# Hidden layer on mirrored token pairs: the first product by 64-row tiles, ReLU as two maxima on VectorE

## The chip, the cores and the metric

One core of one Trainium2 chip. The kernel before took 452.25 us (median of two runs, 452.08 to 452.43).

Engines are called as the profile calls them: PE is TensorE, PEld its weight loads, DVE is VectorE, ACT is ScalarE, POOL is GpSimd, SP is SyncE.

## The reference

```python
x = inputs['x']                                # (8, 3136, 256) float32
X = np.fft.fft(np.fft.fft(x, axis=1), axis=2).real   # real part of a 2-D transform
h = X.transpose(0, 2, 1) @ U @ V               # rank 32, along the sequence
u = X + h.transpose(0, 2, 1)
out = u + np.maximum(u @ w_ch1, 0.0) @ w_ch2   # 256 -> 1024 -> 256
```

Batches are taken in four pairs. The transform is done by matmuls in two stages (the *first transform* over one factor of the sequence, the *lines* over the other), then comes the hidden layer. Two facts carry the change. Token k and its mirror, token -k modulo 3136, have transforms that agree in the even part over the 256 features and differ in the sign of the odd part. And relu(A+B) = max(A, -B) + B, relu(A-B) = max(A, B) - B.

## The kernel before

A chunk is 512 tokens. It is taken through the first product (W1), a ReLU that ScalarE writes straight into the operand of the second product, the second product (W2) with the residual added in the same accumulator, and a drain, which takes the sum out of PSUM (the memory that matmuls accumulate in). A step of the next pair's first transform is also shown.

```python
def mlp1(ch, jp):                                   # a quarter of a chunk's first product
    ...
    ps = psh.tile([P, 2, 512], FP32, tag="h", name="hps")
    for i in range(2):
        j = ...
        for blk in range(2):                        # 128 rows each: the whole array
            nc.tensor.matmul(ps[:, i, 0:n], (W1p if ch.sg > 0 else W1m)[jp // 2][:, blk, j],
                             q[:, blk, c0:c0 + n], start=(blk == 0), stop=(blk == 1))
    nc.scalar.activation(ch.h[:, 2 * jp:2 * jp + 2, 0:n], ps[:, :, 0:n], AF.Relu)

def mlp2(ch, t, last=False):                        # second product of 128 tokens
    ...
    for j in range(JT):                             # JT = 8 blocks of 128 hidden units
        nc.tensor.matmul(ps, ch.h[:, j, t * P:(t + 1) * P], W2[:, j, :], ...)
        if j < 2:                                   # residual
            nc.tensor.matmul(ps[:, j], q[:, j, tk], (Bp if ch.sg > 0 else Bm)[:, j], ...)
    ...
    def drain():
        nc.scalar.copy(om[:, 0:n], ch.po[:, 0:n, 1])
        nc.vector.tensor_tensor(ob[:, 0:n, 0:P], ch.po[:, 0:n, 0], om[:, 0:n], op=AL.add)
        nc.vector.tensor_tensor(ob[:, 0:n, P:D], ch.po[:, 0:n, 0], om[:, 0:n], op=AL.subtract)
        ...                                         # stores

def step(g):                                        # first transform of the next pair, 16 steps
    ps = psd.tile([P, 2, D], FP32, tag="ps", name="ps")    # one PSUM tile a step
    ...                                             # matmuls into ps
    evac(z[...], ps[:])                             # always ScalarE
```

## Time and profile before

| | before |
|---|---|
| time, us | 452.25 |
| PE, DVE, ACT busy, share of the span | 95%, 50%, 65% |
| granted PE clock | 1.00 throughout |
| start to first hidden product, us | 28.0 |
| pairs one, two, three, us | 114.0, 102.0, 102.3 |
| last pair and tail, us | 103.3 |

The groups of the page that the change replaces (columns: line, engine, operation, output and inputs, shapes, count, then busy us and mean ns of one, then the engine's idle time before them and what ended most of it):

```profile
L385 ACT ACTIVATE hT<-hps 128x1024 bf16<-128x1024 f32 (+1 forms) x208 | 202.6, 976 | 109.6 <-PE hps L383 100.9
L394 PE MATMUL ops<-W,hT 128*128 128x256 bf16 x1568 | 224.7, 273 | 1.2 <-DVE ob L408 1.0
```

ScalarE waits for TensorE before its ReLUs (100.9 us in all), while TensorE waits 1.2 us in the whole run before second products. Everything queues behind TensorE, so that is the engine that one wants to relieve.

### The profile page before, as it was taken

The page shows a single profiled execution, that of the slowest core. Times are in us where ns is not written, and L with a number is a line of the kernel's source. Part 1 is how long each engine was busy: PE and PEld are TensorE (multiplying, and loading weights), DVE is VectorE, ACT ScalarE, POOL GpSimd, SP SyncE. Part 2 cuts the span into 40 slices and gives each one's busy share as a digit, 9 for nine tenths or more (in the row PEclk, how much of TensorE's full clock was granted, in tenths as well). Part 3 has the DMA queues.
Part 4 walks back from the last instruction along what each step waited for, and adds up shares of the span by engine and source line. Part 5 has one row for each costly group of instructions (what it writes and reads, how often), then busy time and mean ns, then how long its engine had stood idle before and what let it go on. Part 6 is the DMA issues. An engine that isn't in the chain of part 4 may idle for free.

```text
span 449.6 us, 10536 instructions
## 1 busy us (share of the span) xinstructions
PE 426.6 (95%) x4158; PEld 308.7 (69%) x4221; DVE 224.6 (50%) x541; ACT 290.3 (65%) x402; POOL 142.6 (32%) x180
## 2 busy tenths in 40 slices
PE   3889997999999999999999999999999999999995
PEld 1756665776777777767867777777867777667764
DVE  7873686874344466373354467363354344222222
ACT  5886754676565567777465667777466655666662
POOL 7465455851330545550510545360500000000000
PEclk9999999999999999999999999999999999999999
DMA  8749753875592657863772647773662222222323
GB/s 149 159 138 168 211 162 109 254 181 176 162 231 66 171 137 214 235 207 96 171 195 62 171 113 238 223 200 101 165 141 66 71 65 66 72 72 74 85 54 93
DMA packets 59761, 64.34 MB, mean 143 GB/s; under 512 B 12950, under 2 KB 52672, under 8 KB 59552
## 3 DMA queue, kind: packets, MB, share of 16 engines
q1 hardware_dynamic: 50000, 42.68, 36.8%
q0 software_dynamic: 7232, 14.30, 13.5%
q10 hardware_dynamic: 2480, 6.69, 4.0%
q8 instruction: 33, 0.54, 0.5%
q14 instruction: 16, 0.13, 0.1%
HBM read 34.62 MB, written 32.19 MB: 149 GB/s over the span
## 4 chain that ended last, share of the span: by engine, by line
PE 84%; DVE 5%; DMA 3%; issue 3%; POOL 2%; ACT 1%; SPq 1%; DVEq 0%; ACTq 0%; POOLq 0%
PE ops L394 35%; PE hps L383 35%; PE ps L322 5%; PE ops L397 4%; PE ps L185 2%; DMA out_dram<-ob 2%; PE teps L284 1%; DMA w_f<-in_moe_w_ch_dram 1%; SPq L412 1%; DVE g L76 1%; ACT hT L385 1%; PE w1ps L679 1%; DVE q L76 0%; DVE ta L447 0%; DVE ob L407 0%
## 5 line engine op out<-in xcount | busy, mean ns | idle before, releaser
L385 ACT ACTIVATE hT<-hps 128x1024 bf16<-128x1024 f32 (+1 forms) x208 | 202.6, 976 | 109.6 <-PE hps L383 100.9
L394 PE MATMUL ops<-W,hT 128*128 128x256 bf16 x1568 | 224.7, 273 | 1.2 <-DVE ob L408 1.0
L394 PEld LDWEIGHTS <-hT 128*128 128x128 bf16 x1568 | 145.1, 98 | 35.0 <-DVE ob L408 0.8
L76 DVE CAST q<-ps 128x512 bf16<-128x512 f32 (+3 forms) x121 | 65.2, 560 | 83.8 <-PE ps L322 80.1
L383 PE MATMUL hps<-q,W1p 128*128 128x512 bf16 (+1 forms) x420 | 103.2, 355 | 2.6 <-DVE q L76 0.5
L407 DVE TENSOR_TENSOR ob<-ops,om 128x256 f32<-128x256 f32 (+1 forms) x102 | 41.8, 410 | 117.7 <-ACT om L406 116.3
L383 PE MATMUL hps<-q,W1m 128*128 128x512 bf16 x351 | 95.7, 379 | 2.1 <-ACT hT L385 0.5
L144 POOL TENSOR_TENSOR y<-xa,xb 98x510 f32<-98x510 f32 (+1 forms) x48 | 60.9, 1289 | 108.5 <-DMA xa<-in_x_dram 84.2
L383 PEld LDWEIGHTS <-W1p 128*128 128x128 bf16 x448 | 40.3, 98 | 27.3 <-issue 2.2
L383 PEld LDWEIGHTS <-W1m 128*128 128x128 bf16 x384 | 35.3, 98 | 26.5 <-issue 1.4
L397 PEld LDWEIGHTS <-q 128*128 128x128 bf16 x392 | 38.3, 98 | 21.6 <-issue 0.9
L406 ACT COPY om<-ops 128x256 f32<-128x256 f32 (+1 forms) x102 | 37.3, 366 | 14.4 <-PE ops L394 7.8
L306 POOL COPY g<-te 64x1024 int32<-64x1024 int32 (+1 forms) x23 | 24.9, 1122 | 56.3 <-DVE te L270 51.7
L408 DVE TENSOR_TENSOR ob<-ops,om 128x256 f32<-128x256 f32 (+1 forms) x102 | 41.2, 404 | 0.0
L73 ACT CAST z<-ps 128x512 bf16<-128x512 f32 x48 | 28.2, 587 | 17.2 <-PE ps L185 16.4
L397 PE MATMUL ops<-Bp,q 128*128 128x128 f16 x200 | 38.4, 219 | 0.0
L322 PE MATMUL ps<-T,g 128*128 128x128 bf16 (+3 forms) x400 | 36.9, 218 | 0.5 <-ACT q L73 0.3
L397 PE MATMUL ops<-Bm,q 128*128 128x128 f16 x192 | 36.9, 219 | 0.0
L322 PEld LDWEIGHTS <-g 128*128 128x128 bf16 (+1 forms) x400 | 29.4, 98 | 5.0 <-issue 0.6
L99 POOL DMA_INDIRECT xb<-in_x_dram,idx x24 | 25.1, 1044 | 5.4 <-issue 4.5
L134 DVE TENSOR_TENSOR yb<-y 98x508 bf16<-98x508 f32 (+1 forms) x24 | 21.1, 879 | 0.1
L76 DVE COPY g<-zt 32x400 bf16<-32x400 bf16 (+3 forms) x45 | 17.2, 383 | 6.3 <-ACT zt L73 5.7
(136 smaller groups left out, 208.1 us busy)
## 6 DMA issues: line engine op xcount, KB each, us to landing
out_dram<-ob SPq DMA_DIRECT2D x389, 64.0 KB
xa<-in_x_dram SPq DMA_DIRECT2D x24, 392.0 KB
zturn<-z ACTq DMA_DIRECT2D x9, 512.0 KB
g<-zturn SPq DMA_DIRECT2D x3, 800.0 KB
g<-zturn SPq DMA_DIRECT2D x3, 544.0 KB
X<-in_x_dram POOLq DMA_DIRECT2D x4, 384.0 KB, 7.7
X<-in_x_dram POOLq DMA_DIRECT2D x2, 744.0 KB
zturn<-z ACTq DMA_DIRECT2D x3, 448.0 KB
```

What stands on the lines that cost most here:

```text
L73: nc.scalar.copy(o, i)
L76: nc.vector.tensor_copy(o, i)
L99: nc.gpsimd.indirect_dma_start(out=ck.xb.rearrange("p l d -> p (l d)"), out_offset=None, in_=x_g, in_offset=bass.IndirectOffsetOnAxis(ap=i ...
L144: nc.gpsimd.tensor_tensor(ck.y[:, l0:l1, 1:256], ck.xa[:, l0:l1, 1:256], rb[:, l0:l1, 255:0:-1], op=AL.add)
L322: nc.tensor.matmul(o, lt, r, start=st, stop=True, skip_group_check=True)
L383: nc.tensor.matmul(ps[:, i, 0:n], (W1p if ch.sg > 0 else W1m)[jp // 2][:, blk, j], q[:, blk, c0:c0 + n], start=(blk == 0), stop=(blk == 1))
L385: nc.scalar.activation(ch.h[:, 2 * jp:2 * jp + 2, 0:n], ps[:, :, 0:n], AF.Relu)
L394: nc.tensor.matmul(ps, ch.h[:, j, t * P:(t + 1) * P], W2[:, j, :], start=(j == 0 and (t % 2 == 0 or last)), stop=(j == JT - 1), skip_group ...
L397: nc.tensor.matmul(ps[:, j], q[:, j, tk], (Bp if ch.sg > 0 else Bm)[:, j], start=False, stop=False, skip_group_check=True)
L406: nc.scalar.copy(om[:, 0:n], ch.po[:, 0:n, 1])
L407: nc.vector.tensor_tensor(ob[:, 0:n, 0:P], ch.po[:, 0:n, 0], om[:, 0:n], op=AL.add)
L408: nc.vector.tensor_tensor(ob[:, 0:n, P:D], ch.po[:, 0:n, 0], om[:, 0:n], op=AL.subtract)
```

## The change

The intent is to relieve it. A mirrored pair of tokens needs the even product A and the odd product B only once, each over its own 128 of the 256 transformed features. They run as 64-row tiles of the array, two at a time. VectorE forms the two maxima, the second written in reversed token order. The linear rest, plus or minus B times W2, joins the residual through a table W1 x W2 that is built at the start (`RR`). The low-rank term no longer goes through q but enters as its own small products (`TE`, `TK`). The second product is also cut into 64-row tiles, in two phases, so that the array stays in one tiling mode. The core of the diff:

```diff
-        for blk in range(2):
-            nc.tensor.matmul(ps[:, i, 0:n], (W1p if ch.sg > 0 else W1m)[jp // 2][:, blk, j], q[:, blk, c0:c0 + n], ...)
-    nc.scalar.activation(ch.h[:, 2 * jp:2 * jp + 2, 0:n], ps[:, :, 0:n], AF.Relu)
+        for blk in range(2):
+            for s in range(2):                      # even part on rows 0-63, odd part on rows 64-127
+                lt = W1z[64:P, ja] if s and blk == 0 else W1p[c][64 * s:64 * s + 64, blk, jc]
+                nc.tensor.matmul(o[s], lt, q[64 * s:64 * s + 64, blk, c0:c0 + w], ...)
+        for b, a, n, v in ch.parts:                 # low-rank term
+            for s in range(2):
+                nc.tensor.matmul(o[s][:, a:a + n], TE[ch.p % 2][b][64 * s:64 * s + 33, ja],
+                                 VZ[64 * s:64 * s + 33, b, v:v + n], ...)
+    ab = apool.tile([P, 3, 512], BF16, tag="ab", name="ab")      # apool: bufs=2
+    nc.scalar.copy(ab[:, 0:2], ps[:])                            # A and B
+    ts(ab[:, 2], ab[:, 1], -1.0, None)                           # -B, VectorE
+    nc.vector.tensor_tensor(h[:, 1], av[0], av[2], op=AL.max)
+    nc.vector.tensor_tensor(flip[0][:, :, ::-1], flip[1], flip[2], op=AL.max)   # mirrored
...
+    def phase(ha):                                  # second product, half the rows for each of two sides
+        ...
+        for j in range(JT):
+            for s, op, half in sides:
+                last = nc.tensor.matmul(op, ch.h[rows[half], s, j, ...], W2[rows[half], j, :], ...)
...
         def step(g):                                # first transform
-            ps = psd.tile([P, 2, D], FP32, tag="ps", name="ps")
+            if g % 2 == 0:
+                pr.s1 = bank2("s1")                 # one tile for two steps
+            ps = pr.s1[:, g % 2].rearrange("p (l d) -> p l d", l=2)
...
-            evac(z[...], ps[:])
+            evac[g % 2](z[...], ps)                 # ScalarE for even g, VectorE for odd g
```

Cut here: the set-up of the low-rank tables (`v_lines`, `v_copy`, `te_turn`, `te_hidden`, `te_direct`), the product W1 x W2 (`w1_turn`, `product`), the lines in row tiles, and the plan that places the next pair's work between chunks.

## The prediction

> **What bounds the kernel now.** I read the page's first part, then the chain of waits, then the busy table by stretches, then the groups.
>
> ```profile
> PE 426.6 (95%) x4158; PEld 308.7 (69%) x4221; DVE 224.6 (50%) x541; ACT 290.3 (65%) x402; POOL 142.6 (32%) x180
> PE 84%; DVE 5%; DMA 3%; issue 3%; POOL 2%; ACT 1%; SPq 1%; DVEq 0%; ACTq 0%; POOLq 0%
> ```
>
> TensorE is busy 95% of the span and is 84% of the chain that ended last. The stretches, cut at the points where one pair of batches gives way to the next (columns: stretch, its length, then busy us and count of PE, weight loads, DVE, ACT, POOL), say that this holds throughout:
>
> ```profile
> 33.00:137.00 104.00, 99.22 (x1114) 71.57 (x1129) 64.18 (x154) 65.97 (x98) 50.48 (x60) 1.00 0.70 179
> 137.00:241.00 104.00, 103.21 (x904) 75.30 (x917) 52.54 (x116) 69.34 (x95) 37.30 (x38) 1.00 0.59 164
> 345.00:450.00 105.00, 98.53 (x789) 70.62 (x800) 30.06 (x79) 62.00 (x83) 0.00 (x0) 1.00 0.28 72
> ```
>
> The reader should see that a middle pair of about 102 us has TensorE full, VectorE about half used and the clock at 1.00. Busy TensorE time is a modelled union, so I take starts instead. In the timeline of TensorE (start, length, what, count):
>
> ```profile
> 212.48 0.82 PE L394 MATMUL ops<-W,hT 128*128 128x256 bf16 x6
> 213.22 1.32 PE L284 MATMUL teps<-z,UZ 128*64 128x129 bf16 x40
> 214.48 1.04 PE L383 MATMUL hps<-q,W1p 128*128 128x512 bf16 x3
> ```
>
> Six second products cover 0.82 us, of which the last takes 0.27, so one starts every 0.11 us (109 ns in the trace). Likewise 512 columns take 216 ns, 128 take 56, 64 take 28, each with its own weight load hidden. One chunk of 512 tokens is then 16 x 216 (first product) + 4 x (8 x 109 + 2 x 56) (second product and residual) + 16 x 28 (its mixing lines) = 3.45 + 3.94 + 0.45 = 7.83 us. A pair holds 12.25 chunks, 95.9 us, plus 3.6 for the next pair's first transform and 2.7 for other pieces: 102.2, and the trace has pairs starting at 142.0, 244.0 and 346.3. So the sum of streamed columns is the bound, and I can price the change with it.
>
> **What the Trainium skill says.** "TensorE: Matmul & The Clock Gate", Part 3 (row/col tiling), says matmuls on different row groups of the array run at once, the second starting about 4 ns after the first. No run here shows row tiles. The trace shows column tiles: the 40 products of about 128 columns above take 1.32 - 0.22 = 1.10 us, 27.5 ns each, half of 56, so two halves do run together with their weight loads. "TensorEngine Tiling (Array Packing)", Key Properties, says a change of tiling mode drains the array. The trace agrees: 213.22 comes 190 ns after the sixth product's start (213.03) rather than 109, and 214.48 comes about 160 ns after the last tile's start rather than 28, so a round trip costs about 0.2 us. "VectorE: DVE Perf Modes", the perf-mode tier table, gives two-input bf16 in SBUF two elements a cycle and one-input four. The trace has the second: 512 bf16 in 334 ns and a mirrored copy of 1600 in 583 ns, so reversing kept the fast mode. It has no two-input bf16 operation. "SBUF — State Buffer", Who interferes with whom, says a VectorE instruction with two SBUF inputs and a GpSimd read lock each other out. The trace agrees:
>
> ```profile
> L134 DVE TENSOR_TENSOR yb<-y x24: 546/678/2377, 65.5 to 307.1; 98x508 bf16<-98x508 f32 x21, 98x381 bf16<-98x381 f32 x3
> L770 DVE TENSOR_SCALAR W1m<-W1p,sg x4: 334/341/1323, 45.1 to 47.0; 128x512 bf16<-128x512 bf16 x4
> ```
>
> The columns are minimum/median/maximum ns: 678 usually, 2377 at worst, and 341 against 1323, on a fold engine (GpSimd) whose own operations take about 1270.
>
> **The change part by part.** A mirrored token pair has the even half of q in common and the odd half negated. The first product is made once per pair, even part A on array rows 0 to 63 and odd part B on rows 64 to 127; relu(A+B) is max(A,-B) plus B, and the added linear term goes into the residual product. The low-rank term leaves q and becomes a third small product.
>
> TensorE, per 512 tokens. First product: 8 hidden blocks x 3 (two halves of q, one low-rank) pairs of 256 columns = 24 x 109 = 2.62 us, from 3.45, if the two row tiles overlap fully. Second product: cut into the same row tiles, in two phases; a phase is 8 x 109 plus 218 for the wider residual (512 columns against 256), so 4 x 1.09 = 4.36 us, from 3.94: it gets dearer. Mixing lines: 64 columns in row tiles, 16 x 28 / 2, with half of the lines' columns gone, 0.11 to 0.22, from 0.45. Sum 7.11 against 7.83. A pair has 12 such chunks and a small one for line zero: 85.4 + 2.8 = 88.2, from 95.9. Added: hidden and direct low-rank products, per batch 4 x 216 + 2 x (56 + 109), so 2.4 a pair, and about 14 more mode round trips, 2.8. A middle pair becomes 88.2 + 3.6 + 1.8 + 2.4 + 2.8 = 98.8 from 102.2; the last 88.7 from 95.9. The first gains 7.7 and loses about 4 to W1 x W2 and its transposes. All lies on the path: 4 + 3.4 + 3.4 + 7 = about 18 us, 452 to 434 if nothing else binds.
>
> VectorE. Instructions go from 541 to about 1120. Per group of 512 hidden columns it now does a negation (as the 512 bf16 above less its pointer scalar, about 280 ns, plus about 30 because the next one needs it) and two maxima (256 cycles of two elements at 0.96 a ns is 267, plus the 145 that the fold shows above its 529, so 410, of which consecutive ones overlap 84: 326). That is 0.96 us x 50 groups = 48 us a pair. A mirrored copy of q adds 3.4, half the z moves 4.9. Removed: about 24 moves of q at 0.69, leaving 6 at 0.6. So a middle pair has 52.5 - 16.6 + 3.6 + 4.9 + 48.2 + 3.4 + 0.4 = 96 us on VectorE against 98.8 on TensorE, before lockouts. GpSimd folds some 22 us in a pair; if VectorE loses 0.5 us to each of 16, its demand is 104. This is the part that decides.
>
> ScalarE: the relu of 1024 becomes a copy of 1024, count 200 for 208; it gains small copies and loses half of z, so it stays near 71 us a pair, off the path. GpSimd loses the spreads (25 us) it had time for, worth nothing. The stores are unchanged in bytes.
>
> **The rivals.** (1) TensorE stays the bound and row tiles overlap fully: about 434. For it: column tiles do, and the 64-column lines show a weight load every 28 ns, so two loads fit in 109. (2) VectorE becomes the bound while the next pair is folded. Then pair one stays near 113, the middle ones near 104, and only the last gains 7: 28 + 113 + 208 + 89 + 8 = 446 of span, 449 of time, no change to speak of. For it: 96 of 98.8 before lockouts. Against: the folds need not collide each time. (3) The mirrored maximum drops to one element a cycle: 267 ns more x 50 = 13 us a pair on VectorE, about 485. Against it: the reversed copy. (4) Row tiles do not overlap, or all four double banks of the one shared PSUM pool wait for VectorE: over 500. The drain of an output bank now stands behind six maxima in VectorE's order, and the second phase waits for a ScalarE no-op that stands behind a copy of 1 us. Nothing in the profile excludes stalls of 0.3 us there, which 96 phase changes would make 29 us.
>
> **Range and chances.** Between rival 1 (434) and rival 2 (449), with VectorE seldom fully blocked, I choose 441, range 425 to 462: below if lockouts are rare and the maxima are shorter than reckoned, above for phase stalls. A middle of 441 lies just under the 2% line at 443, so 0.55 faster, 0.34 same, 0.11 slower.
>
> **What would show it.** Row overlap: starts of paired products a few ns apart and 109 per pair. Second product: 1.09 us a phase. VectorE: negation near 280, each maximum near 410 (near 680 if one element a cycle), middle pairs near 95 us busy, worst cases over 1 us during folds. TensorE idle before first products, released by ScalarE's copy or VectorE's drain, means rival 2 or 4. The last pair, which has no folds, should be near 89 us whichever of 1 and 2 holds. I am wrong if it isn't, or if middle pairs leave 99 to 104.

## More of the kernel before

The metric is the device time of one execution in microseconds (us).

I cut the span where each pair issues its first hidden product (W1), in every kernel of this study, so that stages can be set side by side. The busy table for the kernel before, cut so (columns: stretch, its length, then busy us and count of PE, PEld, DVE, ACT, POOL, then PE clock, DMA share, GB/s):

```profile
0.00:28.00 28.00, 18.29 (x434) 13.73 (x437) 21.28 (x73) 20.39 (x29) 14.98 (x42) 1.00 0.82 178
28.00:142.00 114.00, 108.40 (x1186) 77.61 (x1204) 71.17 (x164) 72.53 (x105) 55.21 (x65) 1.00 0.65 167
142.00:244.00 102.00, 101.21 (x886) 73.83 (x899) 51.15 (x113) 68.17 (x94) 37.30 (x38) 1.00 0.59 165
346.30:449.60 103.30, 97.22 (x778) 69.53 (x788) 29.85 (x78) 61.08 (x83) 0.00 (x0) 1.00 0.28 72
```

The third column group is the one to remember: VectorE works 71 of 114 us in the first pair and 51 of 102 in a middle one.

## The result, and the profile after

The changed kernel is correct and takes 524.29 us (524.29 and 524.30), against 452.25. The ratio is 1.159, with a 95% interval of 1.154 to 1.164. Ratios in this document are the mean time of one kernel's runs over that of the other's runs of the same rounds, so they are not quite the ratio of the medians quoted beside them.

The page of the changed kernel, its first lines and the shares of the chain that ended last:

```profile
PE 448.1 (86%) x8099; PEld 374.3 (72%) x8101; DVE 428.4 (82%) x1120; ACT 296.6 (57%) x418; POOL 126.7 (24%) x172
PEclk9877999978999999998999999899999999999999
PE 50%; DVE 29%; ACT 9%; DMA 5%; issue 4%; SPq 1%; POOL 0%; DVEq 0%; ACTq 0%; POOLq 0%
```

TensorE has gone from 84% of the chain to 50%, VectorE from 5% to 29%, ScalarE from 1% to 9%. The bound is no longer one engine but a loop through three. The clock row, 9 in every slice before, now has 7s and 8s, most of them in the first third. The groups:

```profile
L424 ACT CAST ab<-hps 128x1024 bf16<-128x1024 f32 x200 | 202.3, 1014 | 145.2 <-PE hps L421 111.6
L474 PE MATMUL ops<-W,hT 64*128 64x256 bf16 x3008 | 205.3, 272 | 2.4 <-DVE hT L428 2.0
L535 DVE TENSOR_SCALAR ab<-ab 128x512 bf16<-128x512 bf16 x200 | 75.9, 380 | 44.6 <-ACT ab L424 43.1
L428 DVE TENSOR_TENSOR hT<-ab 128x512 bf16<-128x512 bf16 x200 | 98.8, 494 | 6.9
L431 DVE TENSOR_TENSOR hT<-ab 128x512 bf16<-128x512 bf16 x192 | 85.6, 446 | 0.0
```

ScalarE's part is nearly unchanged, a pass of about 1 us over 200 blocks rather than 208. The last three lines, 260 us in all, are new work on VectorE. The busy table by pairs:

```profile
0.00:36.60 36.60, 20.06 (x405) 12.70 (x407) 27.62 (x74) 18.85 (x28) 24.52 (x58) 0.89 0.71 152
36.60:187.00 150.40, 125.49 (x2198) 101.34 (x2199) 123.24 (x314) 77.23 (x113) 42.12 (x52) 0.93 0.52 127
187.00:303.40 116.40, 104.95 (x1888) 87.57 (x1882) 100.66 (x255) 68.92 (x97) 30.77 (x32) 0.99 0.55 146
423.50:522.50 99.00, 91.73 (x1756) 86.03 (x1748) 75.30 (x222) 62.71 (x84) 0.00 (x0) 0.99 0.31 74
```

| stretch | before, us | after, us | difference |
|---|---|---|---|
| start to first hidden product | 28.0 | 36.6 | +8.6 |
| pair one | 114.0 | 150.4 | +36.4 |
| pair two | 102.0 | 116.4 | +14.4 |
| pair three | 102.3 | 120.1 | +17.8 |
| last pair and tail | 103.3 | 99.0 | -4.3 |

Half of the loss is in the first pair, which the prediction had treated as the least interesting one. The last pair, which has no next pair to prepare, is the only one that gains.

**TensorE did its part.** The timeline of TensorE in a steady stretch (start, length, line, operation, count):

```profile
250.50 1.03 PE L474 MATMUL ops<-W,hT 64*128 64x256 bf16 x16
251.37 0.27 PE L417 MATMUL hps<-q,W1p 64*128 64x256 bf16 x1
251.37 0.27 PE L417 MATMUL hps<-q,W1z 64*128 64x256 bf16 x1
```

The two row tiles of a pair (the last two lines) start within 10 ns of each other, and sixteen second products take 251.37 - 250.50 = 0.87 us, that is 109 ns for each pair of tiles, what one whole-array product cost before.

**Where TensorE stood still.** I also summed, over a middle pair, the time between the starts of successive TensorE instructions that goes beyond what the first of them streams, by what ended it. In pair two, 97.2 us are streaming and 19.2 are gaps: 7.0 for ScalarE's moves in the first transform, 4.1 for VectorE's drains, 2.5 for ScalarE otherwise, and 5.6 for the rest, mostly changes of tiling mode and small pieces. (The page's own wait list shows less, since it counts only the time after a matmul's modelled end.) The largest item, in the timeline of all engines:

```profile
263.62 0.68 DVE L143 TENSOR_TENSOR yb<-y 98x508 bf16<-98x508 f32 x1
264.22 0.68 DVE L144 TENSOR_TENSOR yb<-y 98x508 bf16<-98x508 f32 x1
264.89 0.42 DVE L502 TENSOR_TENSOR ob<-ops,om 128x256 f32<-128x256 f32 x1
265.23 0.41 DVE L503 TENSOR_TENSOR ob<-ops,om 128x256 f32<-128x256 f32 x1
265.70 0.40 PE L196 MATMUL s<-yb,F 98*128 98x258 bf16 x2 [0.35 <-DVE ob L503]
266.13 0.58 ACT L82 CAST z<-s 128x512 bf16<-128x512 f32 x1 [0.78 <-PE s L196]
266.77 0.38 PE L196 MATMUL s<-yb,F 98*128 98x258 bf16 x2 [0.67 <-ACT z L82]
```

Read it from the top. VectorE is in two folds for the next pair (a fold adds mirrored parts of the input ahead of the first transform), so the drain of an output bank stands behind them; TensorE's first transform starts at 265.70, released by that drain. Its second half could follow at once, but it goes into the other half of the same PSUM tile, and it waits until ScalarE has moved the first half (266.13 to 266.71): 0.67 us of wait and, start to start, 1.07 us instead of the 0.22 that the first half streams. That happens eight times in a pair.

### The profile page after: what moved, and what is told of

Its sections match the earlier page's. It is cut to its first block, busy times and chain, and to the rows that moved or that the text cites. A ratio compares the mean times of both kernels' runs of the same rounds, so it can differ in the third digit from the quotient of the medians.

```text
span 522.5 us, 19249 instructions
## 1 busy us (share of the span) xinstructions
PE 448.1 (86%) x8099; PEld 374.3 (72%) x8101; DVE 428.4 (82%) x1120; ACT 296.6 (57%) x418; POOL 126.7 (24%) x172
## 4 chain that ended last, share of the span: by engine, by line
PE 50%; DVE 29%; ACT 9%; DMA 5%; issue 4%; SPq 1%; POOL 0%; DVEq 0%; ACTq 0%; POOLq 0%
PE ops L474 18%; PE hps L417 11%; PE hps L421 5%; DVE ab L535 5%; DVE hT L431 5%; ACT ab L424 4%; DVE hT L428 4%; DMA out_dram<-ob 3%; PE ops L461 3%; PE s L196 3%; ACT z L82 2%; DVE yb L143 2%; DVE yb L144 2%; DVE ob L502 2%; DVE ob L503 2%
## 5 line engine op out<-in xcount | busy, mean ns | idle before, releaser
L424 ACT CAST ab<-hps 128x1024 bf16<-128x1024 f32 x200 | 202.3, 1014 | 145.2 <-PE hps L421 111.6
L474 PE MATMUL ops<-W,hT 64*128 64x256 bf16 x3008 | 205.3, 272 | 2.4 <-DVE hT L428 2.0
L474 PEld LDWEIGHTS <-hT 64*128 64x128 bf16 x3008 | 156.9, 95 | 15.7 <-DVE hT L428 3.9
L417 PE MATMUL hps<-q,W1p 64*128 64x256 bf16 (+1 forms) x1248 | 150.3, 269 | 9.8 <-DVE ob L503 2.1
L421 PE MATMUL hps<-VZ,TE 33*128 33x256 bf16 (+1 forms) x896 | 119.0, 263 | 0.7 <-DMA VZ<-q 0.7
L535 DVE TENSOR_SCALAR ab<-ab 128x512 bf16<-128x512 bf16 x200 | 75.9, 380 | 44.6 <-ACT ab L424 43.1
L417 PE MATMUL hps<-q,W1z 64*128 64x256 bf16 (+1 forms) x416 | 111.8, 271 | 0.8 <-DVE W1z L535 0.8
L428 DVE TENSOR_TENSOR hT<-ab 128x512 bf16<-128x512 bf16 x200 | 98.8, 494 | 6.9
L417 PEld LDWEIGHTS <-W1p 64*128 64x128 bf16 x1248 | 82.1, 96 | 13.7 <-issue 7.1
L431 DVE TENSOR_TENSOR hT<-ab 128x512 bf16<-128x512 bf16 x192 | 85.6, 446 | 0.0
L454 PE MATMUL ops<-TK,VS 64*128 64x256 f16 x188 | 51.4, 273 | 3.0 <-issue 1.1
L196 PE MATMUL s<-yb,F 98*128 98x258 bf16 (+1 forms) x108 | 19.2, 268 | 21.7 <-ACT z L82 17.7
```

The source lines that it names most:

```text
L417: nc.tensor.matmul(o[s], lt, q[64 * s:64 * s + 64, blk, c0:c0 + w], start=(i == 0 and blk == 0), stop=True, skip_group_check=True)
L421: nc.tensor.matmul(o[s][:, a:a + n], TE[ch.p % 2][b][64 * s:64 * s + 33, ja], VZ[64 * s:64 * s + 33, b, v:v + n], start=False, stop=True, ...
L424: nc.scalar.copy(ab[:, 0:2], ps[:])
L428: nc.vector.tensor_tensor(h[:, 1], av[0], av[2], op=AL.max)
L431: nc.vector.tensor_tensor(flip[0][:, :, ::-1], flip[1], flip[2], op=AL.max)
L454: mm = nc.tensor.matmul(o, VS[0:64, 1 - s, v + t * P:v + t * P + P], TK[p2][b][:], start=start, stop=False, skip_group_check=True)
```

## The experiments

Fifteen kernels were run. All start from the changed kernel. Three explanations were on the table: **waits** that the changed order puts before TensorE (the shared tile above being the largest); **VectorE's load**, near the length of a pair before GpSimd's lockouts are added; and **the start**, with its longer chain of set-up work and its halved clock. The expectations below are quoted. Where one refers to a theory by letter, A is the wait at the shared tile and E the depth of the A/B buffers. Pair times are given in the order one, two, three; the changed kernel has 150.4, 116.4, 120.1. They come from one profiled execution of each kernel, so small differences mean little: in the four variants below that touch only the start or the first pair (GpSimd's block later, idle matmuls, no tables, lighter first pair), pair two lies between 114.8 and 121.4 and pair three between 116.3 and 121.8. The two together are steadier, 234 to 238 against 236.5 in the changed kernel, so the middle pairs are best judged by that sum.

### Middle pairs: the waits

**Both halves of the shared tile computed before either is moved.**

```diff
-            evac[g % 2](z[...], ps)
+            move = lambda: evac[g % 2](z[...], ps)
+            if g % 2 == 0:
+                pr.held = move
+                return
+            pr.held()
+            move()
```

> The changed kernel with one reordering: both halves of a first-transform tile are computed before either half is moved out (in the changed kernel the second half's products wait for ScalarE's move of the first, 24 times, about 0.84 to 1.35 us each, 21.5 us in all). Theory A (that wait lies on the path): 524 becomes 502 to 508, middle pairs 116 to 120 us become about 109 to 113. Theory B (VectorE's queue is what paces the first three pairs, the wait is only cover): less than 6 us gained, the idle time of TensorE reappears behind VectorE's output additions.

520.0 us (519.0 to 521.0), ratio 1.147, correct; pairs 148.1, 113.8, 116.4. Who waited for what at the first transform, in the changed kernel, then in this one (columns: us, times):

```profile
  DVE ob L503: 10.6, 16
  ACT z L82: 17.7, 24
```

```profile
  DVE ob L508: 16.8, 18
```

The wait for ScalarE's move is gone altogether, as intended, and the wait for VectorE's drains has grown from 10.6 to 16.8 us over the run. So the wait was real, but behind it stood the next one: taking 7.0 us out of each middle pair won 2.6 and 3.7, that is 6.3 of 14.0.

**All moves of the first transform and of the lines on ScalarE.**

```diff
-            s1 = list(s1_steps(nx, [copy_act, copy_dve]))
+            s1 = list(s1_steps(nx, [copy_act, copy_act]))
...
-        both = [copy_act, copy_dve]
+        both = [copy_act, copy_act]
```

> The changed kernel with all moves of z and q on ScalarE instead of half on VectorE: 48 moves of 0.60 us, 29 us off VectorE, 23 to 28 us onto ScalarE, which is 57% busy. Theory B: 505 to 515. Theory A: 520 to 528, as the second half's products still wait for ScalarE.

518.55 us (515.8 to 521.3), ratio 1.144, correct; pairs 147.4, 116.1, 120.1. The middle pairs did not move at all. Shifting these moves from VectorE to ScalarE is worth nothing there, so VectorE's sum by itself does not set the time of a middle pair.

**No folds on GpSimd** (wrong result).

```diff
-        ck.y = ypool.tile([PR, 4, D], FP32, tag="y", name="y")
-        ...                                    # three GpSimd additions
+        ck.y = ck.xa
```

> Wrong result on purpose: the changed kernel without the folds on GpSimd (VectorE folds the loaded rows directly). Theory C (lockouts between GpSimd's reads and VectorE's two-input operations cost the middle pairs 8 to 10 us each): VectorE operations over 1 us vanish, middle pairs fall to 106 to 110, the whole to about 500. If lockouts are rare, the whole falls by under 5 us; then the folds matter neither way.

514.32 us (512.3 to 516.3), ratio 1.134; pairs 152.0, 110.5, 111.3. The first maximum's durations, in the changed kernel and in this one (minimum/median/maximum ns, then first and last start in us):

```profile
L428 DVE TENSOR_TENSOR hT<-ab x200: 424/426/1402, 42.1 to 515.0; 128x512 bf16<-128x512 bf16 x100
```

```profile
L423 DVE TENSOR_TENSOR hT<-ab x200: 424/426/447, 43.2 to 507.1; 128x512 bf16<-128x512 bf16 x100
```

The long ones vanish with GpSimd's folds, so the lockouts are shown; in pair two VectorE's busy time falls from 100.7 to 89.5 us with the same 255 operations. The folds cost the two middle pairs 5.9 and 8.8 us, 14.7 together, somewhat less than was expected; pair one gained nothing from their absence.

**No negation, both maxima of A and B** (wrong result).

```diff
-        ts(ab[:, 2], ab[:, 1], -1.0, None)
...
-        nc.vector.tensor_tensor(h[:, 1], av[0], av[2], op=AL.max)
+        nc.vector.tensor_tensor(h[:, 1], av[0], av[1], op=AL.max)
```

> Wrong result on purpose: the changed kernel without the negation (the first maximum takes A and B instead of A and -B). Takes about 0.31 us x 200 = 63 us off VectorE, nothing else. Theory B (VectorE paces the first three pairs): 524 becomes 480 to 495, middle pairs near 105. Theory A (the first-transform wait and the startup chain): its waits stay, so 514 to 522. The last pair, which has TensorE to itself, should change by under 1 us under both.

508.67 us (507.9 to 509.4), ratio 1.122; pairs 142.3, 112.5, 114.4 (9.6 less in the two middle ones together), and 99.9 for the last with the tail. VectorE's busy time falls by 54 us, from 428 to 374, and the time by 16. Of the figures expected neither came: VectorE's work matters, but under a third of what was taken away shows.

**Negation and maximum in one instruction.**

```diff
-        ts(ab[:, 2], ab[:, 1], -1.0, None)
...
-        nc.vector.tensor_tensor(h[:, 1], av[0], av[2], op=AL.max)
+        nc.vector.scalar_tensor_tensor(h[:, 1], av[1], -1.0, av[0], op0=AL.mult, op1=AL.max)
```

> The changed kernel with negation and first maximum made one VectorE instruction (B times -1, maximum with A). If that instruction takes one element a cycle it lasts about 680 ns against 283 + 424 and its wait, so VectorE saves little (0 to 40 ns x 200) and the time stays within 1%. If two elements a cycle, 420 ns, it is as the kernel without negation: about 508.

520.82 us (517.3 to 524.3), ratio 1.154, correct; pairs 142.0, 117.2, 117.4. The instruction's durations:

```profile
L427 DVE SCALAR_TENSOR_TENSOR hT<-ab x200: 671/692/1761, 43.4 to 507.4; 128x512 bf16<-128x512 bf16 x100
```

692 ns for 512 elements against 293 + 426 = 719 for the two that it replaces: about one element a cycle. It is a way to have one instruction fewer, not to have less work, and the first of the two outcomes expected came. The runs spread by 7 us, and the difference to the changed kernel lies inside that.

**Four A/B buffers in place of two**, on top of the previous edit (three slots of four would not fit in memory).

```diff
-        ab = apool.tile([P, 3, 512], BF16, tag="ab", name="ab")
+        ab = apool.tile([P, 2, 512], BF16, tag="ab", bufs=4, name="ab")
```

> The one-instruction form of negation and maximum, with four instead of two buffers between ScalarE's copy and VectorE's maxima (a third buffer's worth of space is freed by the form). Theory E (the depth of that buffer couples the engines: ScalarE waits for VectorE's maxima, so it frees no bank): first pair 142 becomes 130 to 136 and the middle pairs 117 become 112. Theory F (VectorE's amount of work and its order decide): within 4 us of the 521 of the same form with two buffers.

524.82 us (523.3 to 526.3), ratio 1.156, correct; pairs 147.7, 120.6, 117.4. Nothing was gained. ScalarE waiting for a free buffer is a sign that VectorE is late, not the reason.

**Three together: the shared tile, no negation, no folds** (wrong). The edits are those of the first, third and fourth experiments above:

```diff
-            evac[g % 2](z[...], ps)
+            ...                                # held, then both moves
-        ts(ab[:, 2], ab[:, 1], -1.0, None)     # and max(A, B) twice
+        ck.y = ck.xa                           # in place of the GpSimd additions
```

> Wrong result on purpose: the three earlier edits together (both halves computed before a move, no negation, no folds on GpSimd). Each alone took 3 to 16 us. If the middle pairs' excess over the 98.8 us of streamed columns is made only of the first-transform wait (7.0 us a pair) and of waits for VectorE's queue, one hiding behind the other, the middle pairs fall from 116 and 120 to 98 to 101 us and the whole to about 480; if something in TensorE itself (mode changes, weight loads of row tiles) costs more than reckoned, they stay above 105.

481.92 us (479.0 to 484.9), ratio 1.068; pairs 132.4, 102.4, 103.4. The second pair of this kernel:

```profile
171.60:274.00 102.40, 100.29 (x1887) 87.24 (x1881) 75.45 (x205) 68.80 (x97) 0.00 (x0) 1.00 0.50 134
```

This is the run that settles the middle pairs. With 25 us less on VectorE, no lockouts and no wait at the shared tile, TensorE is busy 100.3 of 102.4 us again, and the pair takes what it took before the change. Separately the three edits won 6.3, 9.6 and 14.7 us in the two middle pairs, sum 30.6; together 30.7 of the 32.2 that were lost there, so no fourth cause is needed. And it shows how little there was to win: 97.2 of streaming and 5.6 of mode changes and small pieces make 102.8, so with nothing else in the way TensorE would have gained nothing in a middle pair.

### The start

**GpSimd's second block of the low-rank table moved behind the second batch's loads.**

```diff
-    v_lines(nc.gpsimd, 9, 17)
     v_copy(1, 9)
...
+    v_lines(nc.gpsimd, 9, 17)
     front.__exit__(None, None, None)
```

> The changed kernel with GpSimd's first table block moved behind the loads of the second batch, so that it does not run beside VectorE's table work at 26 to 33 us, where an equality of 128 elements takes 2.06 us and two additions take 3.92. Theory C2 (lockout in the startup chain): those fall to about 0.35 and 1.4 us, the first product starts at 31 to 33 us instead of 36.6, TensorE's gap of 3.1 us shrinks below 1 us and its granted clock from 34 to 42 us is 1.0 instead of 0.5; the whole falls by 5 to 10 us. If the chain is bound by other things (loads of W1), by under 2 us.

VectorE's operations at the start, in the changed kernel, then in this one:

```profile
26.75 2.06 DVE L535 TENSOR_SCALAR eye<-jf,pf 128x128 bf16<-128x128 f32 x1
28.73 3.92 DVE L760 TENSOR_TENSOR VZ<-uv 32x512 bf16<-32x512 f32 x2
```

```profile
27.75 0.28 DVE L535 TENSOR_SCALAR eye<-jf,pf 128x128 bf16<-128x128 f32 x1
27.96 2.14 DVE L760 TENSOR_TENSOR VZ<-uv 32x512 bf16<-32x512 f32 x2
```

The lockout is gone and the first hidden product starts at 33.6 us in place of 36.6. But pair one becomes 152.8, the second pair starts at 186.4 in place of 187.0, and the time is 521.47 us (518.2 to 524.7), ratio 1.156, correct. What the start won, pair one gave back.

One trace alone would not show that the edit does this, because GpSimd's block meets other operations of VectorE in each execution. In twelve of the thirteen kernels that have it in its old place, it meets the operations shown or the row copies just before them (with negation and maximum in one instruction, six copies took 7.17 us in place of 3.67), and the first hidden product starts at 36.6 to 40. In the thirteenth, the one without tables below, it began behind them, and the start was 31.9. In the three kernels that have the edit it was 31.5 to 33.9.

**38 idle matmuls of 256 columns, to keep the clock up.**

```diff
+    fill = bank_d("fill")
+    for i in range(24):
+        nc.tensor.matmul(fill[:, 0], idle[:, 0:P], idle[:, P:384], start=True, stop=True)
     te_turn(first, [0])
+    for i in range(14):
+        nc.tensor.matmul(fill[:, 0], idle[:, 0:P], idle[:, P:384], start=True, stop=True)
```

> The changed kernel with 24 and 14 idle 256-column products put where TensorE stands idle around 30 to 35 us; they compute nothing that is used. Theory D (the halved clock at 34 to 43 us follows from that idle time): the granted clock there is 1.0, the first chunk takes about 6 us instead of 8.4, the whole falls by 2 to 5 us although TensorE has more to do. If the clock falls for another reason it stays at 0.5 and nothing is gained.

526.0 us (523.3 to 528.7), ratio 1.166, correct; the first hidden product starts at 39.8. The stretches of 2 us around the start, in the changed kernel, then in this one (the clock is the third number from the end):

```profile
30.00:32.00 2.00, 0.05 (x1) 0.00 (x0) 2.00 (x1) 0.00 (x0) 1.93 (x2) 1.00 0.07 16
38.00:40.00 2.00, 2.00 (x22) 1.40 (x20) 1.88 (x1) 0.66 (x1) 1.93 (x2) 0.50 1.03 132
42.00:44.00 2.00, 2.00 (x32) 1.76 (x32) 1.93 (x7) 1.89 (x3) 1.84 (x5) 0.86 0.75 106
```

```profile
34.00:36.00 2.00, 2.00 (x12) 1.37 (x10) 0.11 (x1) 0.00 (x0) 1.56 (x3) 0.51 0.89 166
36.00:38.00 2.00, 2.00 (x20) 1.60 (x19) 0.54 (x2) 0.22 (x1) 1.92 (x5) 1.00 0.77 160
40.00:42.00 2.00, 0.07 (x1) 0.00 (x0) 1.99 (x3) 0.04 (x1) 1.93 (x2) 1.00 1.45 197
44.00:46.00 2.00, 2.00 (x29) 1.91 (x26) 1.93 (x7) 1.72 (x3) 0.00 (x0) 0.50 0.00 0
```

TensorE's idle stretch from 30 us on is followed by a halved clock, until about 42. In the filled kernel it was halved from 29 to 36 (an idle stretch of 2.35 us had ended at 26.6), came back to 1.00 while the filling ran, which had begun at 33.0, and was halved again after the next idle stretch, at 40 to 42. In both traces the halved clock follows idle time; a gain from filling it is not shown.

### The first pair

**No tables for the linear rest** (wrong): the turning of W1 and the product W1 x W2 are taken out.

```diff
-            at[0].append(lambda: (w1_turn(0), w1_turn(1)))
...
     def product():
-        ...                                    # 16 matmuls, G and RR made of them
+        nc.gpsimd.memset(G[:].bitcast(FP32), 0.0)
+        nc.gpsimd.memset(RR[0][:].bitcast(FP32), 0.0)
+        nc.gpsimd.memset(RR[1][:].bitcast(FP32), 0.0)
```

> Wrong result on purpose: the changed kernel without the startup work that the linear rest needs (transposes of W1, W1 times W2, and the tables G and R made from it on VectorE); G and R are zeros. Takes away about 5 us of TensorE and 4 us of VectorE at 41 to 57 us, where TensorE waits 2.9 us for W2 and 1.4 us for G. If this chain is what makes the second chunk last 17.0 us, that chunk falls to 9 or 10, the halved clock there goes, and the first pair falls from 150 to 140 to 143 us. If the first pair is held by VectorE's queue in general, it falls by under 4.

521.37 us (518.1 to 524.6), ratio 1.150. The first product starts at 31.9, pair one takes 150.9. The chain of tables, which I had priced at about 4 us, is not what makes the first pair long; how much it adds is not settled, since the slow clock differs too: (1 - clock) x time in pair one is 15.1 us here and 9.8 in the changed kernel. What the trace shows in its stead is VectorE: it is in the fold of W2 (38.93 to 41.46), the negations and maxima of the first chunk stand behind it, and ScalarE's copy of the third block then waits 4.8 us for a buffer that the maxima have not yet read.

**Lighter first pair**: also no fold of W2 and no row copies for the second batch (wrong).

```diff
-                quarter_rows(g, st.zt, 4 * r - 4, [copy_dve] * 8)
...
-            at[0].append(lambda: w2_fold(0))
-            at[1].append(lambda: (w2_fold(1), v_copy(1, 9, None)))
+            at[0].append(lambda: nc.gpsimd.memset(W2[:].bitcast(FP32), 0.0))
+            at[1].append(lambda: v_copy(1, 9, None))
```

> Wrong result on purpose: the kernel without the W1 times W2 tables, and besides without VectorE's fold of W2 and without its 58 row copies of the second batch in the first pair; zeros stand there. That takes about 4 + 3.8 + 10 to 15 us off VectorE's 123 in that pair. Theory F (VectorE's side work stands ahead of the maxima in its queue, so it delays the main line): first pair 151 becomes 130 to 138, middle pairs unchanged. If TensorE's own pieces hold the first pair, it stays above 145.

517.42 us (515.5 to 519.3), ratio 1.140; pairs 141.7, 121.4, 116.3. VectorE's busy time in pair one falls from 123 to 111 us, by 12 where 18 to 23 had been reckoned, and the pair by 9, to between the two outcomes expected.

**The same, and the three edits of the middle pairs** (wrong); the edits are as shown there.

> Wrong result on purpose: the previous kernel with the three edits for the middle pairs as well (no negation, no GpSimd folds, both halves before a move). Middle pairs 102 to 103 as with the three edits alone, first pair 115 to 122, whole 462 to 472. If the first pair then comes to 114 or less, its excess is settled as VectorE's work on the main line; if it stays near 130, something else holds it.

481.57 us (481.1 to 482.1), ratio 1.061; pairs 135.8, 103.1, 103.9.

```profile
39.90:175.70 135.80, 118.42 (x2164) 96.81 (x2165) 83.02 (x219) 74.25 (x110) 34.21 (x43) 0.95 0.69 180
```

VectorE has only 83 of 135.8 us to do here and TensorE is at 118, and still the pair is no shorter than the 132.4 of the kernel with the three edits alone. So VectorE's load explains a part of the first pair's loss, and then stops explaining it.

**Everything suspected taken off at once** (wrong): the three edits, no tables, the GpSimd block later, the second batch's row copies on ScalarE, the low-rank products one slot later.

```diff
-                quarter_rows(g, st.zt, 4 * r - 4, [copy_dve] * 8)
+                quarter_rows(g, st.zt, 4 * r - 4, [copy_act] * 8)
...
-                at[e + 1 + b].append(lambda b=b: (te_hidden(nx, b), te_direct(nx, b)))
+                at[e + 2 + b].append(lambda b=b: (te_hidden(nx, b), te_direct(nx, b)))
```

> Wrong result on purpose: no negation, no GpSimd folds, no W1 times W2, both halves before a move, GpSimd's table block later, row copies on ScalarE, low-rank hidden product one slot later. It asks how far the changed kernel could come with its waits removed. Middle pairs about 99 to 101, first pair 120 to 125, whole 460 to 470: still not below 452, because TensorE's own work is only about 4 us a pair less than before. If it falls below 450, the waits alone decide against the change.

486.92 us (484.5 to 489.4), ratio 1.074; pairs 146.0, 101.5, 103.1. It is not better than the three edits alone, and pair one, expected at 120 to 125, is 13.6 us longer than there. The row copies on ScalarE are a part of that: the ScalarE no-op that hands an output bank from the first phase to the second held TensorE for 6.4 us in five places, and in three of them (3.5 us) it stood right behind these copies. No run takes them alone. In the changed kernel itself that no-op costs 1.2 us in the whole run.

### The other half of the change, and the best that came of it

**The second product on the whole array**, with the residual and low-rank products as they are.

```diff
-                m = mlp2(prv, t, not prv.mini)
-                if not prv.mini:
-                    m.phase(0)
+                m = mlp2(prv, t, False)
...
-            if m is not None and not prv.mini:
-                m.phase(1)
```

> The changed kernel with the second product on the whole array (128 rows) for all chunks, as the kernel before has it, instead of cut into row tiles. Each pair of token tiles then takes 22 x 109 = 2.40 us instead of 2.18, and a change of tiling mode each way, about 0.2 us, 96 times: theory says 20 + 20 = 40 us where TensorE is the bound, most clearly in the last pair, which becomes about 9 us longer. If mode changes are free or row tiles lose as much, the last pair changes by under 3 us.

631.98 us (629.4 to 634.5), ratio 1.394, correct. The last pair with its tail, where no next pair is prepared, and two lines of TensorE's timeline where the 64-row first product gives way to the whole array:

```profile
504.70:627.60 122.90, 112.47 (x1270) 75.77 (x1260) 73.73 (x222) 59.31 (x84) 0.00 (x0) 0.98 0.25 59
562.13 0.27 PE L421 MATMUL hps<-VZ,TE 33*128 33x256 bf16 x2
562.34 0.39 PE L483 MATMUL ops<-R,q 128*128 128x256 f16 x2
```

It took 122.9 us against 99.0. I had reckoned with two changes of mode in a slot of 128 mirrored pairs. There are six, since for each of two sides a 128-row residual, a 64-row low-rank term and a 128-row product alternate. There are 24 slots, and a slot streams 22 products of 256 columns in place of 20 pairs of them, 2 x 0.109 x 24 = 5 us in all. If changes of mode were all the rest, a change would take (24 - 5) / (24 x 6) = 0.13 us. The trace shows less: the two starts are 0.21 us apart in place of 0.109, 0.10 us for the change, and the other changes of this pair cost the same within 0.01. So the changes account for about 14 of the 24 us, the columns for 5, and some 5 are waits. The row-tiled second product, dearer in columns, is worth it.

**A mended version**: the shared tile, the fused negation, the GpSimd block later, row copies on ScalarE, low-rank products a slot later, each edited as above.

> A correct version with the mends that the runs suggest: both halves computed before a move, negation and maximum in one instruction, GpSimd's first table block later, the second batch's row copies on ScalarE, the low-rank hidden product one slot later. If the gains add up (4 + 3.5 + 3 + 5 + 4 us) it takes about 505 us; if they hide behind one another, 512 to 518. Faster than the kernel before (452) it cannot be by any theory left.

514.84 us in four runs (512.9 to 517.3), ratio 1.134 (1.129 to 1.140), correct; pairs 156.0, 113.0, 114.4. It is the best correct version that came of this, and it is still slower than the kernel before. No run beat 452.25, wrong results included; the lowest was 479.0.

## Why the prediction was wrong

441 us was predicted, with a range of 425 to 462; 524.29 came. Both things by which it said that it could be told wrong happened: the middle pairs left 99 to 104, and the last pair was not near 89. Step by step:

- **TensorE's price: right for a tile, 4 us short for a pair.** Row tiles overlap fully, 109 ns a pair, as in the first of the rivals' arguments. From the third on, chunks in the last pair follow each other by 7.0 to 7.3 us against 7.11 predicted. A middle pair streams 97.2 us against 98.8 less 2.8, that is 96.0, and its mode changes with small pieces take 5.6 rather than 2.8. That is 102.8 in place of 98.8, so the 3.4 us that a middle pair was to win were not there even without waits. TensorE's work in the last pair took 92.8 us (423.5 to 516.3) against 88.7.
- **VectorE's price: right in the sum.** The negation has a median of 293 ns against "near 280", the maxima 426 and 418 against "near 410" (the fold's surplus is 678 - 529 = 149 ns, not 145; its rate of 0.96 elements a ns agrees with the trace, where 127 elements more take 132 ns longer). A middle pair has 101 us on VectorE against 104 with lockouts, and 89.5 without GpSimd's folds against 96. So the lockouts cost more than the 8 us reckoned: in pair two, 12 of the negations and maxima take over 0.7 us, and all of them together 10.8 us more than at their medians. The negation, with one tensor input, is locked out as well as the maxima with two; L770, which the prediction showed as a case of two inputs, has one tensor input too. The mirrored maximum keeps two elements a cycle, so rival 3 was wrong, and for the reason given.
- **The ScalarE no-op of rival 4** was not the trouble (1.2 us in all). The other half of that rival, the drain standing behind maxima and folds in VectorE's order, was (4.1 us in pair two); its stated time, over 500, was right, but it was given for reasons of which one failed.
- **What failed is the step from sums to a time: "Then pair one stays near 113, the middle ones near 104".** It took a pair as the larger of two engines' sums, VectorE's with lockouts added. The middle pairs took 116 and 120. With TensorE at 97 + 5.6 us and VectorE at 101, each block passes TensorE, ScalarE, VectorE and TensorE again, through queues in which folds, drains and moves stand between. My reading is that a delay on one side cannot be made up on the other when neither has slack; the chain that ended last, half TensorE and nearly a third VectorE, agrees. The experiments give the sizes, for both middle pairs together: 14.7 us by GpSimd's folds and their lockouts, 9.6 by the negation's length, 6.3 by the shared tile, 30.7 with all three taken off, which is nearly all of the 32.2 lost.
- **A wait was missed.** The move of z by turns was priced as load on VectorE (4.9 us), but not that two steps now share one PSUM tile. That stood in the diff. The wait was 7.0 us of gaps in each middle pair, although undoing it returned only 6.3 in the two.
- **The first pair was never summed for VectorE.** "The first gains 7.7 and loses about 4" is TensorE's account alone. VectorE had 71 of 114 us of its own work there, and the new 48 took it to 123. Before, the ReLU did not pass through VectorE, so its set-up work there held up little; now it stands in front of the first hidden blocks. Counted as for pair two, TensorE stands for about 45 us in pair one, the slow clock's share included: 7.5 at the shared tile and the rest in many waits of under 4 us by cause, so no single edit could return it. The 36.4 us lost are only partly explained: the three edits of the middle pairs return 18.0, and making VectorE lighter still returns no more. The halved clock is a part: over the pair, (1 - clock) x time comes to 0.07 x 150.4 = about 10 us (an estimate from the table by pairs), some of it in idle time, against none before. The remainder, some of it in ScalarE's turns through the low-rank tables, I could not divide by experiment, and it stays open.
- **The start was left out.** It went from 28.0 to 36.6 us; between runs of the variants it lay between 31.5 and 40. One cause, GpSimd's lockout, was removed for 3 us there, and the whole time gained nothing that is clear of its spread.

The rival that was nearest in mechanism, the second, had the right engine and a right cause in the lockouts, and a size of 449. The one nearest in time, the fourth, owed that partly to luck, as said above.

## What to carry to other kernels

When a change sends the main line through one more engine, sum everything that this engine does in *each* stage, set-up included, and not only in the steady one; what was side work becomes something to wait for. Two engines in series that are both near the length of a stage do not give the larger of their sums: here 103 and 101 gave 116 to 120. And size a wait by taking it away, not by its length in the trace: 14.0 us of one, in two pairs, gave back 6.3, because another stood behind it.

## What the Trainium skill lacked or had wrong

- "TensorE: Matmul & The Clock Gate", Part 3, gives a measured speedup for four 32-row tiles but none for two 64-row tiles with their own weight loads. Here sixteen products of 256 columns took 0.87 us, 54 ns each, the full factor of two.
- The same page, Part 1 (what's actually happening), puts both the throttle and its release at about 3.4 us of idle or busy time. The fall agrees in kind, but shorter idle time was enough: after 12 us the changed kernel has six idle stretches of 1.8 to 3.0 us (by modelled ends), and 0.50 came with or after five of them; the kernel before has none over 1.5 us and 1.00 throughout. The gaps of the first pair kept the clock at 0.93 in the mean.
- "TensorEngine Tiling (Array Packing)", Key Properties, says that a change of mode drains the array but gives no time. The runs give about 0.2 us for a round trip between tile widths in the kernel before, and 0.10 us a change, between 64 and 128 rows, in the run with the second product on the whole array.
- "VectorE: DVE Perf Modes", the perf-mode tier table, has no row for the fused scalar-tensor-tensor operation. On 512 bf16 it took 692 ns, about one element a cycle, while the plain maximum of two tensors took 426. The same page's "What auto-detection actually checks" asks for a step of plus or minus one, and the reversed output kept the fast mode as it says: 418 ns.
